# Attention scores, probabilities and AV in plain fp32 with small array tiles, in a transformer block on one core

## The chip, the cores and the metric

The kernel runs on one core of a Trainium2 chip. The metric is the time of one execution on the device in microseconds (us). The profile is one execution as the hardware profiler recorded it.

## The reference

One transformer block on 2,048 tokens of width 448: a layer norm, attention over a sliding window of 256 keys with 16 heads of 28 channels, a residual sum, a second layer norm, and a gated feed-forward layer of width 1,792 with a second residual sum. All inputs and the output are fp32.

```python
def _A_ref(x, wqkv, wo):
    H = 16; Dh = D // H; W = 256
    q, k, v = ...                       # from x @ wqkv
    scores = einsum("bhqd,bhkd->bhqk", q, k) * (Dh ** -0.5)
    mask = (idx[:, None] - idx[None, :] >= 0) & (idx[:, None] - idx[None, :] < W)
    scores = where(mask, scores, -1e9)
    p = softmax(scores, axis=-1)
    o = einsum("bhqk,bhkd->bhqd", p, v)
    return o.transpose(0, 2, 1, 3).reshape(B, S, D) @ wo
x = A_x
h = x + _A_ref(_layernorm(x), A_wqkv, A_wo)
h2 = h + ((gelu(n @ w_gate) * (n @ w_up)) @ w_down)      # n = _layernorm(h)
```

## The kernel before

**Fast fp32 by splitting.** The kernel works in two kinds of matmul. A tile of type F32R is streamed once; to keep fp32 accuracy a value is split into a rounded part ("hi", `to_hi`, on ScalarE) and the rest ("lo", `to_lo`, on VectorE), and a product is the sum of hi x hi, hi x lo and lo x hi. A tile of type F32 is streamed as plain fp32.

**The blocks.** Attention is cut into `NB` = 16 blocks: `B = 4 * c + g`, where c is a chunk of 512 tokens and g one of four groups of four heads. A block has 512 queries and, through the window, up to 768 keys: those of its chunk and the last 256 of the chunk before. The four blocks of the first chunk have no chunk before; they are called first blocks below, the other twelve later blocks.

**What a block does.**

- `project_tile(c, m)` makes q or k of a group for one chunk in 11 split matmuls of 512 columns (L714). Seven tiles m serve four groups, because each tile of 128 columns holds 112 of its own and 16 of the fourth group's k. The result is split by ScalarE and VectorE and written to DRAM by two pairs of DMAs (`put`, L725 and L727).
- `loads(B)` brings q and k back (L747) so that a head has 84 rows: hi and lo parts in three row groups, so that one F32R matmul gives the whole split product. Twelve more rows are zero and eight carry the maxima.
- `scores(B, i, j)` (L765): for query tile i of 128 and head j, one matmul of 84 rows by up to 384 keys; VectorE adds a mask and takes each query's maximum (`most`, L769).
- `maxima(B)` (L796): the maxima are split, transposed by one matmul, and copied by ScalarE into rows 96 to 103 of q, four copies a block (`put`, L424).
- `probs(B, m, o)` (L838): for key tile m the product is computed again, now with keys on the partitions, 104 rows, so that the maximum is subtracted by the matmul; ScalarE takes the exponential into `pp` (L842).
- `select(B, m, o)` (L857): POOL zeroes what the window excludes in the tiles on its edges.
- `attend(B, ms, at)` (L876): AV in plain fp32, 128 rows of keys by 29 columns (28 channels and a column of ones for the sum), four heads side by side in the array at columns 0, 32, 64 and 96, all into one bank.
- `drain(B)` transposes AV on VectorE, divides, transposes back and splits; `output(p, c)` (L936) multiplies two blocks by Wo and adds to `hres`.

`values` (L660) projects v, `layer_norms` prepares the tokens. The feed-forward layer (L1191, L1179, L1386, L1462) follows; its weights are prepared by VectorE, ScalarE, POOL and DMA while attention runs, and its first matmuls (L1191) begin at 265 us.

**The order.** No engine's order is written by hand. Every piece of work is an `op(engine, cost, latency, key, ...)` in a list; `Lists.run` then simulates the engines with these costs, and at each step gives an engine the ready piece with the lowest key (16 keys are one block). It also hands out the eight PSUM banks of 128 x 512: `allowed(kind)` lists the banks that a kind of work may take. Scores use banks 0 and 1, probabilities 2 and 3, AV bank 4, projections and other work 5 to 7. `TURN` is the time that the simulation charges when TensorE changes the tiling of its array. The chip executes the order found; all DMAs go through SP's queue in that order.

Of the kernel before, what the change touches and what calls it, by code (L numbers as in the profile page):

```python
# [16 lines left out]
NT = S // 128  # L17
# [10 lines left out]
PPB = 10  # L28
MERGE = (1, 1, 1, 0, 1, 1, 1, 1, 1, 1, 1, 0)
# [7 lines left out]
LAG_P = 13.5  # L37
LAG_V = 12.0
# [38 lines left out]
PKL = 2  # L77
# [4 lines left out]
PKS = 3  # L82
POOLED = (3,)
PKX = (2, 3)
# [8 lines left out]
TURN = (0.19, 0.09, 0.09)  # L93
# [24 lines left out]
class Lists:  # L118
# [47 lines left out]
    def run(self, allowed, idle):  # L166
# [23 lines left out]
        def start_of(e, o):  # L190
# [6 lines left out]
            for b in o.banks:  # L197
                if b.k is None:
                    ks = [k for k in allowed(b.kind) if bank_free[k] is not None]
# [79 lines left out]
def block_kernel(ctx: ExitStack, tc, x, wqk_in, wv_in, wo_in, gu_in, rest_in, cw_in, down_in, out):  # L279
# [10 lines left out]
    def f(ap):  # L290
# [10 lines left out]
    one_r = pool.tile([128, 128], F32R, name="one")  # L301
# [11 lines left out]
    mx = pool.tile([128, 4, 4], F32, name="mx")  # L313
    mhl = [mhl_m[:, 128 * i:128 * i + 128] for i in range(2)]
    rcp = [pool.tile([128, 16], F32, name=f"rcp{i}") for i in range(2)]

    pool.tile([128, 32], F32, name="pad2")

    qk_d = [[[dram.tile([GF, 3, 512], F32, name=f"{'qk'[i]}{g}_{c}") for i in range(2)] for c in range(CS)]
            for g in range(NG)]  # L320
# [16 lines left out]
    pp_m = lp.tile([128, 4 * PPB * 128], F32, name="pp")  # L337
# [21 lines left out]
    rq = [m.rearrange("p (j t) -> p j t", j=4) for m in rqs]  # L359
    rk = [m.rearrange("p (j t) -> p j t", j=4) for m in rks]  # L360
# [11 lines left out]
    pk = proj_m[:, 3584:5632].rearrange("p (a t) -> p a t", a=4)  # L372
# [3 lines left out]
    wo_raw = raw_m[:, 1024:1472]  # L376

# [7 lines left out]
    def WVRAW(p, b):  # L385
        return span("pp", 7 * p + 1.75 * b, 3.5)
# [3 lines left out]

    def PK(a):
        return span("proj", 3584 + 512 * a, 512)
# [164 lines left out]
    def start():  # L557
# [35 lines left out]
        def const_pick():  # L593
            nc.gpsimd.memset(e8, 0.0)
            for i in range(2):
                nc.gpsimd.affine_select(e8[96:104, 0:4], e8[96:104, 0:4], pattern=[[-1, 4]],
                                        compare_op=OP.not_equal, fill=1.0, base=-4 * i, channel_multiplier=1)

        op("pool", 0.85, 0.9, -100.5, const_pick, (), ["e8"], port=True)
        for i in range(2):  # L600
            op("pool", 0.1, 0.1, -30, lambda i=i: nc.gpsimd.memset(f(mhl[i]), 0.0), (), [("mh", i), ("ml", i)])
        op("act", 0.2, 0.3, -99, lambda: to_hi(one_r, ident), ["ident"], ["one"])

        op("dve", 1.1, 1.15, -99, lambda: nc.vector.memset(f(rqs[0][64:96, 0:1024]), 0.0), (), [("zq", 0, 0)])
        op("act", 1.45, 1.55, -97, lambda: nc.scalar.activation(
            rks[0][64:96, 1536:3072], e8[64:96, 0:1].to_broadcast([32, 1536]), AF.Copy), ["e8"], [("zk", 0, 1)])
# [4 lines left out]
    def constants(after):  # L611
        def const_mask():
            nc.gpsimd.memset(mask, 0.0)
            nc.gpsimd.affine_select(mask[:, 0:128], mask[:, 0:128], pattern=[[1, 128]], compare_op=OP.is_gt,
                                    fill=-BIG, base=0, channel_multiplier=-1)
            nc.gpsimd.affine_select(mask[:, 256:384], mask[:, 256:384], pattern=[[-1, 128]], compare_op=OP.is_ge,
                                    fill=-BIG, base=0, channel_multiplier=1)

        for u, i in ((0, 0), (1, 0), (1, 1)):
            o = 1536 * i  # L620
            op("pool", 1.35, 1.4, (-99, 0)[u], lambda u=u, o=o: nc.gpsimd.memset(f(rks[u][64:96, o:o + 1536]), 0.0), (),
               [("zk", u, i)], after=after)
        for u, i in ((0, 1), (1, 0), (1, 1)):
            o = 1024 * i
            op("pool", 0.95, 1.0, (-98, 0)[u], lambda u=u, o=o: nc.gpsimd.memset(f(rqs[u][64:96, o:o + 1024]), 0.0), (),
               [("zq", u, i)], after=after)
        for u in range(2):
            for j in range(4):
                src = e8[96:104, j:j + 1].to_broadcast([8, 768])
                if j < 2:  # L630
                    op("dve", 0.55, 0.54, (-96, 0)[u] + j, lambda u=u, j=j, src=src: nc.vector.tensor_copy(
                        rk[u][96:104, j], src), ["e8"], [("pick", u, j)], port=True, after=after)
                else:
                    op("act", 0.75, 0.85, (-96, 0)[u] + j, lambda u=u, j=j, src=src: to_hi(rk[u][96:104, j], src),
                       ["e8"], [("pick", u, j)], after=after)
# [43 lines left out]
    pks, ring = [0], [0]  # L679

    def pk_at():
        n = pks[0]
        pks[0] += 1
        if n in PKX:
            m, o, name = pp_m, 1792 + 1024 * PKX.index(n), "pp"
        else:
# [1161 lines left out]
```

## Time and profile before

| | |
|---|---|
| median of 3 runs | 695.22 us (695.12 to 695.36) |
| span of the profiled execution | 693.2 us |
| that execution's own time beside its span | not given; the runs' median stands 2.0 us above the span |
| TensorE busy | 683.7 us |
| VectorE, ScalarE, POOL busy | 540.9, 399.7, 194.2 us |
| matmul records | 5,534 |
| granted TensorE clock | 1.000 |

A row of the profile names a line of the kernel (L765), an engine (PE is TensorE, PEld its weight loads, DVE VectorE, ACT ScalarE, SP the DMA queue), an operation, the tile written and the tiles read, and a shape. `bank<-rk,rq 84*128 84x384 f32 x224 | 72.9, 348` is a group of 224 matmuls with 84 rows and 128 columns of weights and 384 streamed columns, which kept the engine busy for 72.9 us, 348 ns each. A plain fp32 matmul leaves two records for one instruction of the code: AV has 352 matmuls and 704 records. In a timeline a row is a start, a duration and a piece of work; like pieces that follow one another are merged (x8).

### The profile page before, as it was taken

To read this page: it belongs to the slowest core of one execution; us is meant where nothing else is said; L and a number is where in the kernel's file an instruction comes from. 1 tells how busy PE (TensorE), PEld (TensorE's weight loads), DVE (VectorE), ACT (ScalarE), POOL (GpSimd) and SP (SyncE) were. 2 spreads that over 40 slices of the span, in tenths; PEclk is the share of its full clock that TensorE was granted. 3 is DMA by queue.
4 is the path that set the end of the run, shared out by engine and by line. 5 is a ranking of instruction groups with operands and counts; after the bars stand their busy time and mean duration, and the time that the engine had idled before them with its cause. 6 is when DMAs were issued, how large, how long until landed. Compare 5 with 4: busy or idle time off the path is not lost. (4 is left out here: it accounts for less than half of the span.)

```text
span 693.2 us, 15159 instructions
## 1 busy us (share of the span) xinstructions
PE 683.7 (99%) x5534; PEld 581.8 (84%) x5534; DVE 540.9 (78%) x1362; ACT 399.7 (58%) x837; POOL 194.2 (28%) x318
## 2 busy tenths in 40 slices
PE   8999999999999999999999999999999999999997
PEld 7887888887888887878878887888889889999886
DVE  7977678987897798838896899677757888887744
ACT  7747566876677767667554465544524534545430
POOL 5613554644455446441220120010000210120000
PEclk9999999999999999999999999999999999999999
DMA  9997788887789597844754766414103744443102
GB/s 307 286 298 228 240 214 217 191 235 207 192 215 257 130 270 196 213 153 133 192 112 118 213 173 193 129 40 137 60 14 118 226 134 131 133 148 86 43 15 107
DMA packets 104690, 116.24 MB, mean 168 GB/s; under 512 B 44632, under 2 KB 82392, under 8 KB 104040
## 3 DMA queue, kind: packets, MB, share of 16 engines
q1 hardware_dynamic: 104472, 115.17, 59.3%
q8 instruction: 43, 0.70, 0.4%
q14 instruction: 31, 0.25, 0.1%
q10 hardware_dynamic: 144, 0.11, 0.0%
HBM read 84.97 MB, written 44.47 MB: 187 GB/s over the span
## 5 line engine op out<-in xcount | busy, mean ns | idle before, releaser
L769 DVE CUSTOM_DVE_ANT_0 mt<-bank,mt 128x384 bf16<-128x384 f32 (+2 forms) x256 | 126.1, 525 | 23.2 <-PE bank L765 21.0
L1386 PE MATMUL bank<-xT,proj 64*128 64x512 f32 x645 | 121.0, 388 | 0.0
L842 ACT ACTIVATE pp<-bank 128x384 f32<-128x384 f32 (+1 forms) x188 | 90.2, 528 | 17.8 <-PE bank L838 16.7
L1386 PE MATMUL bank<-xo,proj 64*128 64x512 f32 x456 | 98.4, 388 | 0.3 <-DVE e L1302 0.3
L714 PE MATMUL bank<-xT 128*128 128x512 f32 x308 | 95.3, 397 | 0.0
L1386 PEld LDWEIGHTS bank<-xT,proj 64*128 64x128 f32 x645 | 80.9, 184 | 8.9
L838 PE MATMUL bank<-rq,rk 104*128 104x384 f32 (+2 forms) x352 | 80.9, 303 | 0.0
L765 PE MATMUL bank<-rk,rq 84*128 84x384 f32 (+2 forms) x256 | 80.3, 337 | 0.1
L1462 PE MATMUL bank<-proj,gh 64*128 64x448 f32 x624 | 74.9, 362 | 0.0
L857 POOL TENSOR_SCALAR_AFFINE_SELECT pp<-pp 128x512 f32<-128x512 f32 x96 | 60.5, 649 | 44.8 <-ACT pp L842 43.5
L1462 PEld LDWEIGHTS bank<-proj,gh 64*128 64x128 f32 x624 | 62.6, 184 | 6.3 <-DVE e L1302 0.4
L838 PEld LDWEIGHTS bank<-rq,rk 104*128 104x128 f32 x352 | 58.9, 189 | 10.0 <-ACT pp L842 1.7
L1386 PEld LDWEIGHTS bank<-xo,proj 64*128 64x128 f32 x456 | 59.7, 184 | 7.0 <-DVE e L1302 0.7
L714 PEld LDWEIGHTS bank<-xT 128*128 128x128 f32 x308 | 56.2, 189 | 6.8 <-DVE xT L427 0.4
L1386 PE MATMUL bank<-xT,w 64*128 64x512 f32 x276 | 53.8, 389 | 0.3 <-DVE raw L1398 0.3
L424 ACT ACTIVATE rq<-bank 8x512 fp32r<-8x512 f32 x64 | 37.6, 588 | 27.2 <-PE bank L796 26.3
L765 PEld LDWEIGHTS bank<-rk,rq 84*128 84x128 f32 x256 | 46.9, 189 | 6.7 <-DVE mx L769 1.5
L660 PE MATMUL bank<-proj,xT 128*128 128x448 f32 (+1 forms) x220 | 50.6, 334 | 0.3 <-ACT proj L424 0.3
L1386 PE MATMUL bank<-xo,w 64*128 64x512 f32 x240 | 49.7, 391 | 0.7 <-DVE raw L1398 0.6
L1481 DVE TENSOR_TENSOR hres<-bank,hres 128x448 f32<-128x448 f32 (+1 forms) x85 | 47.0, 609 | 1.0 <-PE bank L1462 1.0
L1301 ACT ACTIVATE e<-bank 1x1 f32<-1x1 f32 x75 | 11.8, 158 | 50.0 <-PE bank L1462 34.8
L1386 PEld LDWEIGHTS bank<-xT,w 64*128 64x128 f32 x276 | 35.8, 184 | 4.3 <-DVE raw L1398 0.7
(212 smaller groups left out, 1384.2 us busy)
## 6 DMA issues: line engine op xcount, KB each, us to landing
rk<-k SPq DMA_DIRECT2D x44, 336.0 KB
rq<-q SPq DMA_DIRECT2D x32, 336.0 KB
gu<-in_gu_dram SPq DMA_DIRECT2D x18, 480.0 KB
proj<-gu SPq DMA_DIRECT2D x24, 288.0 KB
q<-proj SPq DMA_DIRECT2D x12, 448.0 KB
proj<-down SPq DMA_DIRECT2D x22, 224.0 KB
proj<-gu SPq DMA_DIRECT2D x24, 192.0 KB
k<-proj SPq DMA_DIRECT2D x9, 448.0 KB
```

Of the source, the lines that this page charges most:

```text
L424: nc.scalar.activation(dst, src, AF.Copy)
L660: op("pe", mm(224 * n), 0.29 if n == 1 else 0.38, key + a / 16, lambda a=a, h=h, wb=wb, xb=xb: nc.tensor.matmul(bank[b.k][:, 0:224 * n], x ...
L714: op("pe", mm(512) + 0.002, 0.403, key, lambda a=a, h=h, wb=wb, xb=xb: nc.tensor.matmul(bank[b.k], wqk[m][:, h, wb, :], xT[:, xb, cc * 128 ...
L765: nc.tensor.matmul(bank[b.k][:, o:384], rq[u][0:3 * DH, j, i * 128:i * 128 + 128], rk[u][0:3 * DH, j, m0 * 128:(i + 3) * 128], start=True, ...
L769: nc.vector.tensor_tensor_reduce(junk[s % 2][:, o:384], bank[b.k][:, o:384], mask[:, o:384], 1.0, -BIG, OP.add, OP.max, mx[:, i, j:j + 1])
L838: nc.tensor.matmul(bank[b.k][:, n * i:n * i + n], rk[u][0:104, j + i, m * 128:m * 128 + 128], rq[u][0:104, j + i, lo * 128:(hi + 1) * 128] ...
L842: nc.scalar.activation(pp_cols(o, n)[:, j:j + G], bank[b.k][:, 0:G * n].rearrange("p (g t) -> p g t", g=G), AF.Exp, scale=SCALE)
L857: nc.gpsimd.affine_select(a, a, pattern=[[0, 4], [-cm, 128]], compare_op=op_, fill=0.0, base=0, channel_multiplier=cm)
L1301: ways = {"act": (0.08, 0.17, lambda: nc.scalar.activation(e8[0:1, 0:1], bank[b.k][0:1, 0:1], AF.Copy), False), "dve": (0.07, 0.17, lambda ...
L1386: nc.tensor.matmul(bank[b.k], w, xarea(u.cp, xl, xs, side)[:, xk], start=p in (1, 2, 5) and not k and not t, stop=t == 2, tile_position=(6 ...
L1462: nc.tensor.matmul(bank[banks[q].k][:, 0:D], h[oh][0]()[HALF[x], q * 128:q * 128 + 128], d[wh][0]()[HALF[x]], start=not ph and not y and n ...
L1481: op("dve", 0.07 + w * 0.463 / D, 0.163 + w * 0.463 / D, key, lambda: nc.vector.tensor_tensor(hres[:, t, c0:c0 + w], bank[b.k][:, c0:c0 + ...
```

## The change

The products of a head stay unsplit. `project_tile` writes q and k straight from the bank into SBUF (`qT[g]`, `kT[g]`, 32 partitions a head: 28 channels and spare rows), by one copy on ScalarE or VectorE, whichever the planner finds free. The trip through DRAM goes; `loads`, `probs`, `slots` and the split of the maxima go with it. The weights are laid out so that each head's 32 columns hold 28 of its own and 4 of the fourth group's k; four DMAs a tile gather those into `kT[3]`, and one fills row 28 of each head with -1.

Scores and probabilities are computed in steps (`scores_and_probs`). A step uses four banks, one a head, of up to 512 columns; a matmul has 32 rows (a head) and 64 columns of weights, at row 32 j and column 64 h, so that eight fit in the array: four heads by two halves of 64 queries or keys. A step holds the scores of one query tile (320 columns in a later block) and the probabilities of an earlier block's group of pieces. VectorE takes maxima and ScalarE exponentials from the same banks. `stage(s)` runs the score steps of block s with probabilities of blocks s - 2 and s - 1, then AV of block s - 2, then `maxima(s)`: VectorE transposes the maxima, four DMAs write them to DRAM and one reads them into q's row 28.

AV is made of matmuls of 64 rows by 29 columns, at row 64 h and column 32 j, with the two halves in two banks; `drain` adds them. `project(B + 2)` is issued two blocks ahead in place of a whole chunk. A step (a "bin" in the code) may take any of the eight banks.

```diff
-    rks = [p.tile([128, 3072], F32R, name=f"rk{u}") for u, p in enumerate((rp, lp))]
-    rqs = [p.tile([128, 2048], F32R, name=f"rq{u}") for u, p in enumerate((rp, lp))]
+    kT = [rp.tile([128, 1024 if g < NG - 1 else S], F32, name=f"k{g}") for g in range(NG)]
+    qT = [lp.tile([128, 512], F32, name=f"q{g}") for g in range(NG)]
...
-TURN = (0.19, 0.09, 0.09)
+TURN = (0.11, 0.11, 0.11, 0.11)
...
     def project_tile(c, m):
...
-        op("act", 0.49, 0.605, key, lambda: to_hi(hl[0], bank[b.k]), (), [tok[0]], b)
-        op("dve", 0.603, 0.698, key, lambda: to_lo(hl[1], bank[b.k], hl[0]), [tok[0]], [tok[1]], b)
...
+        ways = {"act": (0.49, 0.605, lambda: to_hi(dst, bank[b.k]), False),
+                "dve": (0.603, 0.7, lambda: nc.vector.tensor_copy(dst, bank[b.k]), False)}
+        got[B] = op("act", 0.49, 0.605, key, None, (), [main, extra], b, alts=ways)
+        old, new = slice(512 * c, 512 * c + 512), kT[NG - 1]
+        for j in range(4):
+            dma(key + 1, 8, lambda j=j: nc.sync.dma_start(new[32 * j + 4 * m:32 * j + 4 * m + 4, old], dst[32 * j + DH:32 * j + 32]),
+                [extra, "neg"], [("k3", c, m, j)], cost=0.45)
+        if s:
+            dma(key + 2, 8, lambda: nc.sync.dma_start(dst[DH:128:32], new[DH:128:32, old]), ["neg"], [extra], cost=0.45)
...
+    PIECES = {"A": (4, 5, 0, 1, 5), "B": (6, 7, 2, 3, 5), "C": (2, 9, 0, 5, 3), "D": (8, 3, 4, 0, 4), "E": (0, 11, 0, 7, 1),
+              "F": (10, 1, 6, 0, 2), "A1": (4, 5, 0, 1, 3), "B1": (6, 7, 2, 3, 3), "A2": (4, 5, 3, 4, 2), "B2": (6, 7, 5, 6, 2),
+              "d": (8, 9, 4, 4, 4), "f": (10, 11, 6, 6, 2)}
...
+    def scores_and_probs(key, ss, gs):
+        banks = [Bank("bin") for j in range(4)]
...
+        def part(B, h, j, kh, u, n, at, probs):
+            rows = slice(32 * j, 32 * j + DH + probs)
+            dst = HALF[h]
+            if probs:
+                work.append((j, dst, at, n, keys_of(B, kh, 1)[rows], q_of(B)[rows, 64 * u:64 * (u + n)], h))
+                return
+            cuts = [(kh, n)]
+            if block(B)[1] == 2 and B % 4 < NG - 1 and kh < 4 < kh + n:
+                cuts = [(kh, 4 - kh), (4, n - 4 + kh)]
+            for kh, n in cuts:
+                work.append((j, dst, at, n, q_of(B)[rows, 64 * u:64 * u + 64], keys_of(B, kh, n)[rows], h))
+                at += 64 * n
...
+        def go():
+            for j, dst, at, n, w, x, h in work:
+                nc.tensor.matmul(bank[banks[j].k][dst, at:at + 64 * n], w, x, start=True, stop=True,
+                                 tile_position=(32 * j, 64 * h), skip_group_check=True)
+        cost = o * 4 / 2400 + 0.03
+        op("pe", cost, cost + 0.2, key, go, reads, [x for G in gs for x in G.span(0, G.w)], banks, tag="bin", mode=3)
+
+        def most(B, i, o, n, j, hs, b):
+            n, lo = 64 * n, 320 - 64 * n
+            def go():
+                u = B % 2
+                nc.vector.tensor_tensor_reduce(junk[j % 2][hs, lo:320], bank[b.k][hs, o:o + n], mask[hs, lo:320],
+                                               1.0, -BIG, OP.add, OP.max, mx[u][hs, 4 * j + i:4 * j + i + 1])
...
+        def exp(G, o, j, b):
+            op("act", 0.065 + G.w * 0.00088, 0.16 + G.w * 0.00088, key, lambda: nc.scalar.activation(
+                pp[:, j, G.at:G.at + G.w], bank[b.k][:, o:o + G.w], AF.Exp, scale=SCALE), (), [G.span(0, G.w)[j], *ser(b)], b, tag="exp")
...
+    def select(G, key):
...
+        for (ke, ko, ue, uo, n), at in G.pieces:
+            for h, kh, u in ((0, ke, ue), (1, ko, uo)):
+                for v_, cm, op_ in ((kh - 4, -1, OP.is_ge), (kh, 1, OP.is_gt)):
+                    if u <= v_ < u + n:
...
     def maxima(B):
...
+        op("dve", 0.1, 0.2, key, lambda: nc.vector.transpose(mxT[u], mx[u]), al, [("mxT", u)], port=True)
+        for a in range(4):
+            dma(key, 2, lambda a=a: nc.sync.dma_start(mx_d[u][0:16, 32 * a:32 * a + 32], mxT[u][32 * a:32 * a + 16]), [("mxT", u)],
+                [("mxd", u, a)], cost=0.45)
+        dma(key, 8, lambda: nc.sync.dma_start(qT[g][DH:128:32], mx_d[u][0:16].rearrange("(j i) t -> j (i t)", i=4)),
+            [("mxd", u, a) for a in range(4)], [("qx", g)], cost=0.45)
+
+    def stage(s):
+        old = groups[s - 2][-2:] if s > 1 else []
+        new = groups[s - 1] if s else []
...
+        elif s >= 4:
+            part = [G for G in new[:-2] if G.w < 512]
+            todo = [([(s, 0)], old[0:1]), ([(s, 1)], old[1:2]), ([(s, 2)], part[0:1]), ([(s, 3)], part[1:2]),
+                    ([], [G for G in new[:-2] if G.w == 512])]
...
     def attend(B):
...
+            for h, j, kh, lo, hi, o in work:
+                nc.tensor.matmul(bank[banks[h].k][32 * j:32 * j + DH + 1, 64 * lo:64 * hi],
+                                 v[HALF[h], at_v(4 * c - 2 + kh // 2), 4 * g + j, :],
+                                 pp[HALF[h], j, o:o + 64 * (hi - lo)],
+                                 start=(h, j) not in seen_, stop=True, tile_position=(64 * h, 32 * j), skip_group_check=True)
...
     def drain(B):
-        op("dve", 0.63, 0.72, key, lambda: nc.vector.transpose(oblk, bank[b.k]), (), ["oblk"], b)
+        op("act", 0.49, 0.605, key, lambda: to_hi(oblk[:, lo:512], bank[by.k][:, lo:512]), (), ["oblk"], by)
+        op("dve", 0.605, 0.702, key, lambda: nc.vector.tensor_tensor(oT, bank[bx.k], oblk, op=OP.add), ["oblk"], [tok], bx)
+        op("dve", 0.63, 0.72, key, lambda: nc.vector.transpose(oblk, oT), [tok], ["oblk"], port=True)
...
     def allowed(kind):
...
+            return [7, 6, 5, 4] + ([3, 2, 1, 0] if not left["bin"] or kind in ("v", "ln1") and L.fresh("bin") else [])
+        if kind in ("last", "att"):
+            return [5, 4, 3, 2, 1, 0, 6, 7]
+        if kind == "bin":
+            return [0, 1, 2, 3, 4, 5, 6, 7]
```

In `PIECES` an entry names the key units of 64 in the even and the odd half, the first query unit of each, and the number of query units.

More of the change, by code (lines that the diff above doesn't have):

```diff
@@ L198, in start_of @@
                 if b.k is None:
-                    ks = [k for k in allowed(b.kind) if bank_free[k] is not None]
+                    ks = [k for k in allowed(b.kind) if bank_free[k] is not None and k not in [x for _, x in got]]
                     if not ks:
@@ L851, in select @@
[L851 to L862 removed]
+        if kh < 4:
+            c, kh = c - 1, kh + 8
@@ L1679, in free, with project @@
         op("py", 0, 0, 0, lambda: None, (), [name], after=ops)
+    def project(B):
+        c, g = divmod(B, 4)
+        for m in range(2 * g, min(2 * g + 2, WT)):
+            project_tile(c, m)
     ln1(0)
@@ L1742, in block_kernel @@
     down_set(0, 0, DKEY)
-    op("py", 0, 0, 0, open_late, (), ["fp"], after=[o for tag in ("att", "task", "exp", "score", "prob", "most", "tr", "rx") for o in L.all[tag]])
+    op("py", 0, 0, 0, open_late, (), ["fp"], after=[o for tag in ("att", "task", "exp", "bin", "most") for o in L.all[tag]])
     exps.extend(L.all["exp"])
```

453 lines of the change are left out of this document (188 added, 265 removed).

## The prediction

> **What bounds the kernel now.** I read the page from the top: the busy shares, then the slices, then the chain that ended last.
>
> ```profile
> span 693.2 us, 15159 instructions
> ...
> PE 683.7 (99%) x5534; PEld 581.8 (84%) x5534; DVE 540.9 (78%) x1362; ACT 399.7 (58%) x837; POOL 194.2 (28%) x318
> ...
> PE   8999999999999999999999999999999999999997
> ...
> PEclk9999999999999999999999999999999999999999
> DMA  9997788887789597844754766414103744443102
> ```
>
> TensorE is busy from the first slice to the last at full clock, and no other engine comes near. The chain of waits at the end is all feed-forward, which the change leaves alone, so I read attention by stretches instead.
>
> ```profile
> core 0: us, PE busy (x) PEld busy (x) DVE busy (x) ACT busy (x) POOL busy (x), PEclk, DMA share, GB/s
> ...
> 25.00:310.00 285.00, 284.87 (x2022) 234.33 (x2025) 225.59 (x738) 199.11 (x398) 136.01 (x231) 1.00 0.80 220
> ```
>
> A matmul's record holds its latency, so records overlap and "busy" could hide gaps. The timeline of TensorE decides, by start to next start.
>
> ```profile
> 203.72 0.34 PE L838 MATMUL bank<-rq,rk 104*128 104x384 f32 x1
> 203.89 0.84 PE L714 MATMUL bank<-xT 128*128 128x512 f32 x3
> 204.57 0.34 PE L838 MATMUL bank<-rq,rk 104*128 104x384 f32 x1
> 204.75 0.51 PE L765 MATMUL bank<-rk,rq 84*128 84x384 f32 x2
> 205.10 0.34 PE L838 MATMUL bank<-rq,rk 104*128 104x384 f32 x1
> ...
> 205.93 0.40 PE L838 MATMUL bank<-rq,rk 104*128 104x256 f32 x2
> 206.16 0.34 PE L765 MATMUL bank<-rk,rq 84*128 84x384 f32 x1
> ...
> 207.57 0.56 PE L838 MATMUL bank<-rq,rk 104*128 104x128 f32 x4
> 207.97 0.39 PE L765 MATMUL bank<-rk,rq 84*128 84x384 f32 x1
> ```
>
> A score of 384 columns takes 0.175 us (204.75 to 205.10, two of them), a probability matmul of 384, 256 or 128 columns 0.17 (203.72 to 203.89), 0.115 (205.93 to 206.16, two) and 0.10 (207.57 to 207.97, four), a projection of 512 columns 0.23 (203.89 to 204.57, three). 0.17 us for 384 columns and 0.23 for 512 are one pace: the array streams without gaps. So here time is TensorE's work, and the change is worth what it takes from or adds to that work, unless it opens gaps.
>
> **The change, part by part. First what TensorE loses.** The counts are those of the groups with forms kept apart.
>
> ```profile
> L765 PE MATMUL bank<-rk,rq 84*128 84x384 f32 x224 | 72.9, 348 | 0.1
> ...
> L838 PE MATMUL bank<-rq,rk 104*128 104x384 f32 x128 | 43.1, 347 | 0.0
> ...
> L838 PE MATMUL bank<-rq,rk 104*128 104x256 f32 x112 | 22.7, 291 | 0.0
> ...
> L838 PE MATMUL bank<-rq,rk 104*128 104x128 f32 x112 | 16.0, 265 | 0.0
> ...
> L876 PEld LDWEIGHTS bank<-pp,v 128*29 128x29 f32 x512 | 15.5, 108 | 16.5 <-issue 12.9 <-POOL pp L857 0.4 <-POOL bnve L449 0.2
> ```
>
> Scores: 224 x 0.175 = 39.2 us, and 32 shorter ones some 3: 42. Probabilities: 128 x 0.17 + 112 x 0.115 + 112 x 0.10 = 46. The transposed maxima (one matmul a block) 1. AV I take from one block:
>
> ```profile
> 211.19 0.68 PE L714 MATMUL bank<-xT 128*128 128x512 f32 x2
> 211.80 0.42 PE L876 MATMUL bank<-side,v 128*29 128x128 f32 x8
> 212.04 2.34 PE L876 MATMUL bank<-pp,v 128*29 128x256 f32 x32
> 214.19 0.40 PE L876 MATMUL bank<-raw,v 128*29 128x128 f32 x8
> 214.52 0.66 PE L838 MATMUL bank<-rq,rk 104*128 104x128 f32 x4
> ```
>
> The projections end at 211.19 + 2 x 0.23 = 211.65; with the entry 0.15 the block's AV takes 2.87 us to 214.52. Twelve blocks like it and four first ones with nine units of keys instead of twelve: 34.4 + 8.8 = 43. Together TensorE loses 132 us.
>
> **What it gains.** AV is already plain fp32 in four tiles side by side: 32 records over 1,280 columns a head take 212.04 to 214.19, 2.15 us, which is 1.68 ns a column with all four heads at once, four times the 0.45 ns of the split matmuls (0.23 us / 512). The new code does all three products in plain fp32, eight tiles at a time: four heads by two halves. By the code a later block has 20 units of 64 keys by 64 queries in each half, 1,280 columns: scores, probabilities and AV cost 2.15 us each, 6.45 together. A first block has 16 units: 5.16. Sum 12 x 6.45 + 4 x 5.16 = 98 us.
>
> Each change of the tiling leaves the array empty for a moment. On the way in that is the 0.15 us above at most, since one of the two projections may have waited; on the way out eight records of 128 columns take 0.21 (1.68 x 128), to 214.40, and the next starts at 214.52: 0.12. I take 0.12 for each, and 0.03 for eight staggered tiles: a visit costs 0.27. The code has 79 steps of scores and probabilities and 16 AV steps. All apart: 26 us; one visit a stage (17): 5. A step waits for banks that VectorE and ScalarE empty, and projections fit between, so I stay near the upper end: 78 visits, 21 us. TensorE gains 98 + 21 = 119 and loses 132: **13 us less** (8 to 29 by the bounds of the visits).
>
> That eight tiles run side by side no row shows. Nearest rows: four column tiles run fully together (above), and two row tiles in the feed-forward:
>
> ```profile
> 653.24 2.06 PE bank L1386 x18
> 655.30 1.21 PE bank L1462 x12
> ```
>
> 18 half-height matmuls of 512 columns in 2.06 us are 0.114 each, half of 0.23: two row tiles overlap fully. I take full overlap for four by two. The Trainium skill, "TensorE: Matmul & The Clock Gate", section "Measured speedup vs the span model", reports a gain of 10.6 with sixteen 32-row tiles, which speaks for it; no run here shows it.
>
> **The other engines.** VectorE: 224 maxima of 384 keys go to 320 (late blocks 192 of them),
>
> ```profile
> 205.13 0.55 DVE L769 CUSTOM_DVE_ANT_0 mt<-bank,mt 128x384 bf16<-128x384 f32 x1
> ...
> 205.61 0.55 DVE L769 CUSTOM_DVE_ANT_0 mt<-bank,mt 128x384 bf16<-128x384 f32 x1
> ...
> L427 DVE TENSOR_TENSOR proj<-bank,proj 128x512 fp32r<-128x512 f32 x21 | 14.4, 688 | 2.8 <-ACT proj L424 2.7
> ...
> L424 ACT ACTIVATE rq<-bank 8x512 fp32r<-8x512 f32 x64 | 37.6, 588 | 27.2 <-PE bank L796 26.3
> ```
>
> 0.48 us (205.13 to 205.61) by 320/384 is 0.40: 192 x 0.08 = 15 us less, but the first blocks' unequal halves need 96 shorter ones for 64: about 6 back. The 28 low parts (0.69 each, 19 us) go; some 9 projection copies (6 us), 16 adds of the two halves (11 us) and 16 small transposes (2 us) come: about 9 us less of 226, in a stretch some 15 us shorter, 80% busy as before. ScalarE loses the 64 puts (37.6 us) and gains 16 copies (10 us). POOL gets twice as many selects of half the length. None of them sets the end.
>
> Queues: SP loses 112 stores and 76 loads of q and k, and gains four small stores per projection tile (112), 21 fills and 5 transfers a block for the maxima (80): 213 for 188. At 0.45 us each (the four loads in the next fence) that is 11 us more on a queue that is not the bound. But it is served in order: a block's gather waits for four stores to land, and the next blocks' fills, Wo's rows and the feed-forward's weights stand behind it.
>
> The maxima's path is the added wait: before, a matmul and ScalarE's puts; now a transpose, four stores, and a gather. A hop by the nearest row:
>
> ```profile
> 0.79 1.81 SPq L561 DMA_DIRECT2D hres<-in_x_dram  x4
> ...
> 3.33 0.63 DVE L459 BATCH_NORM_STATS2 bnst<-hres 128x6 f32<-128x448 f32 x1 [1.35 <-DMA hres<-in_x_dram]
> ```
>
> 2.5 us from issue to use; two hops and five issues are about 7 us. The probabilities that need them are issued from the third step of the next stage on; a block lasts 285/16 = 17.8 us, of which some half lies between. I cost it at nothing, covered by the next block's projections and first two score steps; without cover it costs up to 7 us a block.
>
> At the start q and k no longer go through DRAM and back, and the DMA engines were at 0.9 or more in the first two slices (the digits above); TensorE's first slice is at 8. A slice is 17 us, so 2 to 3 us are idle there. Gain between 0 and 3 us; I take 2.
>
> **Sum.** 693.2 - 13 - 2 = 678 in the span. The median of the runs, 695.22, stands 2.0 above the span; with it **680 us**.
>
> **The rivals.**
>
> The issue of instructions becomes the bound (slower). Each fp32 matmul gives two load and matmul records; AV now needs 128 pairs in 2.15 us, 17 ns each, and two of five steps 48 pairs in 0.86, 18 ns. The sustained pace shown is 8 records in 0.24 us (211.80 to 212.04), 30 ns, which streaming explains too; for four records there is this:
>
> ```profile
> 162.97 0.13 PEld L876 LDWEIGHTS bank<-pp,v 128*29 128x29 f32 x4 [0.20 <-issue]
> ```
>
> Four loads of 0.108 within 0.13 us start 7 ns apart. If 30 ns is the limit, AV costs 3.84 for 2.15 (+1.7), the two steps 1.44 for 0.86 (+0.6 each), the other three +0.1: 3.2 us a later block, 2.4 a first one, 48 in all: **728**. It decides from about 22 ns on, where AV loses 0.7 and the two steps 0.2 each, 15 us over 16 blocks. The 7 ns speak against it; that no run of more than 8 is shown so close speaks for it. The Trainium skill, "TensorE: Matmul & The Clock Gate", section "Wait — 56ns, not 53.3ns?", states that matmuls start no closer than about 25 ns, however short; by that AV would take 3.2 us and the two steps 1.2, 26 us more, 706. The 7 ns of the trace disagree for different tiles, at least in short bursts.
>
> Waits take the gain: a step needs four banks at once and holds them through four maxima (4 x 0.40) and the exponentials, and the maxima come late by DMA. VectorE's 80% speaks for it. 0.7 us a block is 11: **691**.
>
> The eight tiles run in two turns of four: 98 more, **778**. The two overlaps above speak against it.
>
> More steps joined: with one visit a stage 16 us more go, **664**.
>
> **How the numbers follow.** Forecast (671 to 687) 0.58; waits 0.15; issue 0.15, half of it at 22 to 27 ns a pair (about 695 to 712) and half beyond; two turns 0.03; more joined 0.05; the parts cancel 0.04. 0.2% is 1.4 us, about what a measurement of this kernel tells from no change. Faster: 0.58 + 0.05 + 0.13 of the waits = 0.76; same: 0.04 + 0.01 = 0.05; slower: 0.15 + 0.03 + 0.01 = 0.19. The range runs from 667 to 702: it takes in the waits and the lighter part of the issue rival, and leaves out under 2 in 10.
>
> **What would show it.** Right: TensorE still dense from 25 us on; AV steps near 2.15 us and 512-column steps near 0.86; pauses of 0.10 to 0.12 at each change of tiling; feed-forward's first matmul some 15 us sooner, its own length unchanged. Wrong: AV steps of 3 us or more with all tiles starting late (issue); steps of 1.7 us (two turns); TensorE idle with VectorE's maxima or the gather of q's last row as releaser (waits); feed-forward starting sooner but waiting for its weights' splits.

## The result and the profile after

The changed kernel takes 713.64 us (median of four runs, 712.43 to 716.42) beside 695.17 for the kernel before (694.91 to 695.36) on the same chip: a ratio of 1.0264, with a 95% interval of 1.0237 to 1.0291. The predicted 680.0, and its range up to 702, are missed by 33.6 and 11.6 us. The profiled execution took 712.76 us, its span is 710.9.

The head of the page after, with span, busy time of the engines, and slices:

```profile
span 710.9 us, 22675 instructions
...
PE 692.3 (97%) x9106; PEld 566.4 (80%) x9106; DVE 535.9 (75%) x1409; ACT 361.0 (51%) x864; POOL 205.4 (29%) x430
...
PE   9999999999999989899999999999999999999997
...
PEclk9999999999999999899999999999999999999999
```

TensorE's share has fallen from 99 to 97%, and one digit of the clock is an 8. The same stretch as in the prediction, by engine:

```profile
25.00:310.00 285.00, 275.71 (x5238) 199.81 (x5237) 212.61 (x762) 153.15 (x400) 142.81 (x316) 0.99 0.24 60
```

TensorE was busy for 284.87 of these 285 us before; now it is idle for 9.3, and that is a lower bound, since records overlap. DMA's share fell from 0.80 to 0.24: the trip of q and k through DRAM is gone, and bought nothing at the end.

Where the feed-forward layer's half-row matmuls begin, in the timelines of before and then of after:

```profile
274.18 0.96 PE L1179 MATMUL bank<-xT,proj 64*128 64x512 f32 x6
```

```profile
286.96 0.96 PE L1186 MATMUL bank<-xT,proj 64*128 64x512 f32 x6
```

12.8 us later (its whole-row matmuls, the first of the layer, 10.2 later), where the prediction had some 15 sooner. To see what fills the time I sum, over the whole trace, the time from each matmul's start to the next one's start, by the line of the first:

| TensorE's time, us | before | after |
|---|---|---|
| scores, the maxima's transposes, probabilities, AV of before (L765, L796, L838, L876) | 45.6 + 1.5 + 49.6 + 41.3 = 138.0 | |
| steps of scores and probabilities (L773) | | 101.9 |
| AV (L882) | | 39.6 |
| projections, values, outputs, whole-row feed-forward (L714, L660, L936, L1191; after L659, L626, L944, L1198) | 73.2 + 38.2 + 37.0 + 13.2 = 161.6 | 78.6 + 42.4 + 40.5 + 14.9 = 176.4 |
| the rest of the feed-forward layer | 376.5 | 375.8 |
| start | 10.3 | 11.0 |
| sum of these rows (first to last start 686.2 and 704.4; the rest is rounding) | 686.4 | 704.7 |

138.0 us went, 141.5 came, and 14.8 came on lines that the change does not touch. The rest of the feed-forward layer is as long as before.

One step between projections, in the timeline:

```profile
70.14 1.43 PE L659 MATMUL bank<-xT 128*128 128x512 f32 x5
71.50 0.80 PE L773 MATMUL bank<-k,q 28*64 28x320 f32 x16
72.09 0.53 PE L773 MATMUL bank<-q,k 29*64 29x192 f32 x16
72.55 1.66 PE L659 MATMUL bank<-xT 128*128 128x512 f32 x6
...
239.04 2.56 PE L882 MATMUL bank<-pp,v 64*29 64x192 f32 x128
241.53 0.79 PE L773 MATMUL bank<-k,q 28*64 28x320 f32 x16
```

The step takes 1.05 us (71.50 to 72.55) where 512 columns at 1.68 ns are 0.86; a later block's AV 2.49 (239.04 to 241.53) where 2.15 were expected. Eight tiles do run at once, and 128 AV records in 2.49 us are 19.4 ns each, so an issue rate of 25 or 30 ns a pair is not the bound. The Trainium skill, "TensorE: Matmul & The Clock Gate", section "Wait — 56ns, not 53.3ns?", has matmuls start no closer than about 25 ns; for matmuls in different tiles this row disagrees.

What TensorE's weight loads waited for, largest first (us in total, times, longest; rows by "issue", time with no releaser in the profile, and smaller ones left out):

```profile
PEld bank L773 <- ACT pp L789: 11.4, 33, 0.8
PEld bank L659 <- ACT pp L789: 4.3, 4, 2.3
PEld bank L773 <- DVE mx L783: 2.7, 7, 0.8
PEld bank L882 <- POOL pp L814: 2.3, 5, 0.7
PEld bank L659 <- DVE mx L783: 2.0, 1, 2.0
PEld bank L1198 <- DVE mx L783: 1.9, 1, 1.9
...
PEld bank L773 <- DMA q<-mx: 0.8, 1, 0.8
```

Five of these rows, 22.3 us, are waits for a bank that ScalarE's exponentials (L789) or VectorE's maxima (L783) had not emptied. The trip of the maxima over DMA shows 0.8 us.

### The profile page after: what moved, and what is told of

Its sections match the earlier page's. It is cut to its first block, busy times and chain, and to the rows that moved or that the text cites. A ratio compares the mean times of both kernels' runs of the same rounds, so it can differ in the third digit from the quotient of the medians.

```text
span 710.9 us, 22675 instructions
## 1 busy us (share of the span) xinstructions
PE 692.3 (97%) x9106; PEld 566.4 (80%) x9106; DVE 535.9 (75%) x1409; ACT 361.0 (51%) x864; POOL 205.4 (29%) x430
## 5 line engine op out<-in xcount | busy, mean ns | idle before, releaser
L783 DVE CUSTOM_DVE_ANT_0 mt<-bank,mt 128x320 bf16<-128x320 f32 (+4 forms) x288 | 122.8, 448 | 33.9 <-PE bank L773 18.5
L789 ACT ACTIVATE pp<-bank 128x192 f32<-128x192 f32 (+3 forms) x300 | 99.6, 390 | 75.7 <-PE bank L773 49.3
L814 POOL TENSOR_SCALAR_AFFINE_SELECT pp<-pp 64x256 f32<-64x256 f32 x240 | 96.3, 416 | 60.1 <-ACT pp L789 53.0
L659 PE MATMUL bank<-xT 128*128 128x512 f32 x308 | 83.8, 405 | 5.0 <-ACT pp L789 3.4
L659 PEld LDWEIGHTS bank<-xT 128*128 128x128 f32 x308 | 55.1, 188 | 24.8 <-issue 7.9
L773 PE MATMUL bank<-q,k 29*64 29x128 f32 (+4 forms) x1888 | 61.3, 309 | 1.1 <-DVE mx L783 0.6
L773 PE MATMUL bank<-k,q 28*64 28x320 f32 (+4 forms) x1120 | 57.3, 410 | 0.7 <-ACT pp L789 0.6
L773 PEld LDWEIGHTS bank<-q,k 29*64 29x64 f32 x1888 | 40.6, 131 | 16.3 <-issue 3.2
L626 PE MATMUL bank<-proj,xT 128*128 128x448 f32 (+1 forms) x220 | 46.1, 339 | 0.1
L626 PEld LDWEIGHTS bank<-proj,xT 128*128 128x128 f32 x220 | 35.4, 189 | 7.7 <-issue 3.9
L882 PE MATMUL bank<-pp,v 64*29 64x128 f32 (+4 forms) x1888 | 40.7, 312 | 0.5 <-POOL pp L814 0.3
L882 PEld LDWEIGHTS bank<-pp,v 64*29 64x29 f32 x1888 | 34.2, 106 | 8.5 <-issue 3.7
L773 PEld LDWEIGHTS bank<-k,q 28*64 28x64 f32 x1120 | 23.1, 130 | 21.0 <-ACT pp L789 8.6
```

What stands on the lines that cost most here:

```text
L626: op("pe", mm(224 * n), 0.29 if n == 1 else 0.38, key + a / 16, lambda a=a, h=h, wb=wb, xb=xb: nc.tensor.matmul(bank[b.k][:, 0:224 * n], x ...
L659: op("pe", mm(512) + 0.002, 0.403, key, lambda a=a, h=h, wb=wb, xb=xb: nc.tensor.matmul(bank[b.k], wqk[m][:, h, wb, :], xT[:, xb, cc * 128 ...
L773: nc.tensor.matmul(bank[banks[j].k][dst, at:at + 64 * n], w, x, start=True, stop=True, tile_position=(32 * j, 64 * h), skip_group_check=True)
L783: nc.vector.tensor_tensor_reduce(junk[j % 2][hs, lo:320], bank[b.k][hs, o:o + n], mask[hs, lo:320], 1.0, -BIG, OP.add, OP.max, mx[u][hs, 4 ...
L789: op("act", 0.065 + G.w * 0.00088, 0.16 + G.w * 0.00088, key, lambda: nc.scalar.activation(pp[:, j, G.at:G.at + G.w], bank[b.k][:, o:o + G ...
L814: nc.gpsimd.affine_select(a, a, pattern=[[0, 4], [-cm, 64]], compare_op=op_, fill=0.0, base=0, channel_multiplier=cm)
```

## The experiments

Theory: two costs were sized wrongly, the waits for banks (nothing in the forecast) and the visit to a tiling (0.27 us); the other candidates are the maxima's DMA trip, plain work starved of banks, the order of the work, VectorE and ScalarE taking turns at one bank, and the clock. Where a run's order is "made anew", `Lists.run` found another order from changed costs. Ratios are to the kernel before, measured beside each run, with 95% intervals.

**The visit by itself.** A kernel of TensorE alone, on constant data. `NR` is 12, `plain` a matmul of 128x128 by 512 columns, `sc` one of each of the eight tiles of a step; the functions ending in `_s` do the same in the sorted part. The pattern follows again with AV's eight tiles and with the four tiles of before:

```diff
+    for _ in range(NR):
+        run(3, plain)
+        run(1, sc, 0, 320)
+        run(1, sc, 320, 192)
...
+    run(3 * NR, plain_s)
+    run(NR, sc_s, 0, 320)
+    run(NR, sc_s, 320, 192)
...
```

> Not the computation at all: TensorE alone, on constant data, no eviction; the output is zeros. Twelve turns of three plain 512-column matmuls and one run of tiles stand against the same matmuls sorted (36 plain, then the tiles): the difference by 12 is what one change to a tiling and back costs with no wait in it. Three forms: eight 32x64 tiles of 320 and 192 columns; eight 64x32 tiles, four times 256 columns; four 128x32 tiles, four times 256 columns, as before. If a visit costs what the trace of the changed kernel shows (0.11 in, 0.10 for the first round, 0.09 out, 0.105 for the plain matmul after it), the first two forms give 0.40 us a turn. If it costs the 0.27 us of the prediction and the rest in the trace is waiting, they give 0.27. Issue would show in the sorted part: above 0.86 us for the 32 records of one step and above 2.15 for 128 of AV. At the end TensorE is left idle for one to four pairs of VectorE copies, about 1.2, 2.4, 3.6 and 4.8 us, between stretches of 50 plain matmuls: if an idle stretch near 2 us alone lowers the clock, the first leaves it at 1.00 and the others lower it for some microseconds; if the clock drop in the changed kernel had another cause, it stays at 1.00 after all four.

Its timeline (L54, L65 and L74 are the three tilings in turn with the plain matmuls of L45; L48 plain matmuls sorted; L60, L70, L78 the tilings sorted):

```profile
24.96 1.12 PE L54 MATMUL bank<-k,q 28*64 28x320 f32 x32
26.01 0.96 PE L45 MATMUL bank<-y,w 128*128 128x512 f32 x3
26.90 1.12 PE L54 MATMUL bank<-k,q 28*64 28x320 f32 x32
...
44.27 8.35 PE L48 MATMUL bank<-y,w 128*128 128x512 f32 x36
52.55 10.94 PE L60 MATMUL bank<-k,q 28*64 28x320 f32 x384
63.43 0.97 PE L42 MATMUL bank<-y,w 128*128 128x512 f32 x3
```

A turn takes 1.94 us (24.96 to 26.90). Sorted, three plain matmuls take 8.28 / 12 = 0.69 and a step 10.88 / 12 = 0.907, together 1.597. A visit costs **0.343**: 0.143 within the step (1.05 for 0.907) and 0.20 in the three plain matmuls between (0.89 for 0.69). In the single records the first plain matmul behind the tiles takes 0.335 us to the next start, the second 0.229 and the last, ahead of the tiles, 0.327: so 0.105 of the 0.20 lies behind the tiles and 0.095 ahead of them. The other two tilings:

```profile
89.14 0.96 PE L45 MATMUL bank<-y,w 128*128 128x512 f32 x3
90.03 1.96 PE L65 MATMUL bank<-k,q 64*29 64x256 f32 x64
91.92 0.97 PE L45 MATMUL bank<-y,w 128*128 128x512 f32 x3
...
106.57 20.95 PE L70 MATMUL bank<-k,q 64*29 64x256 f32 x768
127.45 0.96 PE L42 MATMUL bank<-y,w 128*128 128x512 f32 x3
...
130.89 0.96 PE L45 MATMUL bank<-y,w 128*128 128x512 f32 x3
131.78 1.93 PE L74 MATMUL bank<-k,q 128*29 128x256 f32 x32
133.65 0.96 PE L45 MATMUL bank<-y,w 128*128 128x512 f32 x3
...
170.26 20.93 PE L78 MATMUL bank<-k,q 128*29 128x256 f32 x384
191.12 11.63 PE L42 MATMUL bank<-y,w 128*128 128x512 f32 x50
```

AV's: 2.78 a turn less 0.69 and 20.88 / 12 = 1.74: 0.35. The old four tiles: 2.76 less 0.69 and 1.738: 0.33. So a visit has one price for all three, between the two that were expected: 0.345 and not 0.27. The 0.40 that I had read from the changed kernel's trace holds another 0.05, because even sorted a step takes 0.907 and not 0.86.

**Short maxima.**

```diff
-                nc.vector.tensor_tensor_reduce(junk[j % 2][hs, lo:320], bank[b.k][hs, o:o + n], mask[hs, lo:320],
+                nc.vector.tensor_tensor_reduce(junk[j % 2][hs, 256:320], bank[b.k][hs, o + n - 64:o + n], mask[hs, 256:320],
```

> VectorE's maxima read the last 64 columns of each row instead of all 128 to 320, so the maximum over the other keys is left out; nothing else is changed, and every engine's instructions stand in the same order. 288 maxima fall from 0.45 us to about 0.2. If TensorE waits for banks that VectorE and ScalarE empty (some 25 us in the trace), 10 to 25 us go: 689 to 704. If the loss lies in the visits alone, under 2 us go: 711 or more.

702.53 us (701.0 to 703.29), ratio 1.0098 (1.0081 to 1.0115): by the ratios 11.5 us of the 18.4 are gone with less work for VectorE. Who waited for VectorE's maxima (L783) in the changed kernel, and then here:

```profile
  ACT pp L789: 24.2, 48
```

```profile
  ACT pp L789: 5.1, 8
```

The exponentials had waited 48 times for a maximum on the same bank; now 8 times. The five rows of waits above (22.3 us) add up to 15.8 here, 6.5 less: the waits are real. The rest is in part the clock: it is granted at 0.999 to 1.000 in these four runs, and at 0.990 to 0.995 in those of the changed kernel (last section). The run also frees VectorE for its other work (212.6 us busy between 25 and 310 us in the changed kernel, 152.6 here), which it can't tell from the emptying of banks.

**Short maxima and short exponentials.**

```diff
-                pp[:, j, G.at:G.at + G.w], bank[b.k][:, o:o + G.w], AF.Exp, scale=SCALE), ...
+                pp[:, j, G.at:G.at + 64], bank[b.k][:, o:o + 64], AF.Exp, scale=SCALE), ...
```

> As the one with short maxima, and ScalarE's exponentials too take only the first 64 columns of each group (the rest of the probabilities is a constant written once near the start); same order. Banks are emptied in well under half the time. Waits on the emptying: all of the 25 us go, and the drop of the clock that follows one of them: 684 to 692, and what is left above the predicted 680 is visits. Visits alone: 709 or more. Issue of instructions: no change, 712 or more.

700.39 us (699.71 to 702.06), ratio 1.0073 (1.0056 to 1.0091). The groups of the two operations here:

```profile
L783 DVE CUSTOM_DVE_ANT_0 mt<-bank,mt 128x64 bf16<-128x64 f32 (+1 forms) x288 | 57.5, 219 | 56.1 <-PE bank L773 38.8
L789 ACT ACTIVATE pp<-bank 128x64 f32<-128x64 f32 x300 | 51.0, 225 | 93.9 <-PE bank L773 81.7
```

With the work of both about halved (122.8 and 99.6 us in the changed kernel) only 2 us more go by the ratios, whose intervals overlap. Neither theory's number is met: 13 of the 25 have gone, a part of them with the clock (1.000 here), and the kernel is still slower than before. The five rows of waits still add up to 11.0 us. By line of TensorE: steps 91.2, AV 37.9, plain attention lines 174.6.

**Its order made anew** with the costs that the traces show, these short ones included (`TURN` 0.16, steps 0.05 and AV 0.07 longer, select 0.415, maxima 0.22, exponentials 0.225), and any bank for plain work.

> Maxima and exponentials both over 64 columns alone (the rest of both is left out), and the order of the work made anew with the measured costs of everything, these short ones among them. With the old order this computation takes 700 us, about 15 of it still waits. If those 15 stay because the order was made for longer evictions, most of them go: 686 to 693. If they are what is left of each bank's way from TensorE over two engines and back, however it is ordered: 697 to 703.

699.1 us (697.24 to 703.47), ratio 1.0063 (1.0037 to 1.009): the interval overlaps that of the run before it. This second order does not take away what is left.

**Any bank for plain work**, and **the order with measured costs**, both with maxima and exponentials whole:

```diff
-            return [7, 6, 5, 4] + ([3, 2, 1, 0] if not left["bin"] or kind in ("v", "ln1") and L.fresh("bin") else [])
+            return [7, 6, 5, 4, 3, 2, 1, 0]
```

> Projections, values and output products may take any of the eight banks, where the kernel leaves them four while tile steps stand open; the order is worked out anew with that. If the plain matmuls are starved of banks (19 us of idle time ahead of the projections), 4 to 10 us go: 704 to 710. If it is the tile steps that wait, for four banks at once, then plain work in their banks makes it no better: 712 to 718. Visits: no change.

714.7 us (712.24 to 716.07), ratio 1.0264 (1.0241 to 1.0286): nothing gained, so nothing shows that the plain work was starved.

> The same computation; the list that orders the work reckons with the costs that the traces show (a change of tiling 0.16 instead of 0.11 us, a step 0.05 and AV 0.07 us more, a select 0.415), any bank for plain work, and steps 3.0 apart with AV two places and projections some places sooner. If the order was at fault, because it was made with costs too low, a part of the 12 us that the short maxima gave comes back without them: 698 to 706. If the waits lie in VectorE and ScalarE taking turns at each bank, whatever the order: 710 to 716.

715.1 us (714.17 to 718.22), ratio 1.0284 (1.0254 to 1.0314). In this trace the steps take less (97.2 us for 101.9) and the plain attention lines more (181.5 for 176.4): the waits moved.

**Short maxima with the order made anew** for them, any bank for plain work:

> The maxima of the last 64 keys alone, as in the run with short maxima (the maximum over the other keys is left out), and an order worked out anew with the measured costs and with these shorter maxima, any bank for plain work, steps 2.0 apart. Waits: some of the 15 us of waits that stay with short maxima go too, and the drop of the clock does not come back: 690 to 700. Visits alone set the time: no better than 702. With all waits gone the lines of TensorE measured one by one give 138 us removed against 101 at the measured pace, 26 of visits: 684 is the floor.

703.0 us (702.4 to 703.76), ratio 1.0104 (1.0083 to 1.0126): as with short maxima in the old order, and above what the waits theory allowed, where visits alone would leave it. By line, steps and AV take less than in the old order (126.4 us for 133.1), the plain attention lines more (178.8 for 174.9), and the drop of the clock came back: half clock for 3.4 us at 324 us, and a mean of 0.994 to 0.996 in the four runs. It was the version that should have beaten both kernels, and it does not.

**Scores and probabilities in banks of their own.**

```diff
-            scores_and_probs(16 * s + (STEP if len(todo) > 4 else 4) * n, *x)
+            at = 16 * s + (STEP if len(todo) > 4 else 4) * n
+            if x[0]:
+                scores_and_probs(at, x[0], [])
+            if x[1]:
+                scores_and_probs(at + 0.5 * bool(x[0]), [], x[1])
```

> One part of the change undone: scores and probabilities do not share banks, each group of four banks holds only scores (VectorE alone empties them) or only probabilities (ScalarE alone); the order is worked out anew. 38 more runs of tiles, 13 us at 0.345 each. If what costs the 28 us of waits is that VectorE and ScalarE take turns at one bank, most of them go and the sum is 700 to 716. If it is the emptying as such, whoever does it, the waits stay and the visits come on top: 722 to 735.

739.52 us (738.65 to 740.24), ratio 1.0624 (1.0598 to 1.065). What the weight loads waited for:

```profile
PEld bank L773 <- DVE mx L783: 14.9, 41, 1.1
PEld bank L773 <- ACT pp L789: 12.1, 32, 1.4
```

The trace has 108 runs of steps for 70 and 33 more changes from whole matmuls to tiles and back: 38 x 0.143 + 33 x 0.20 = 12 us by the visit's price. 13 more are waits: 27.0 us in these two rows for 14.1. No two engines take turns at a bank any more, and the steps wait longer. So taking turns is not needed for the waits. I put them down to there being more groups of four banks to empty; that is argued, not shown.

**No maximum subtracted.**

```diff
-            rows = slice(32 * j, 32 * j + DH + probs)
+            rows = slice(32 * j, 32 * j + DH)
...
-            reads += [("q", G.B % 4), ("qx", G.B % 4), *k_toks(G.B, True)]
+            reads += [("q", G.B % 4), *k_toks(G.B, False)]
```

> The probabilities are taken without row 28, so no maximum is subtracted; the maxima are still computed, transposed and carried by DMA, but no step waits for them. If the trip of the maxima over two DMAs holds the steps up, 5 to 10 us go (704 to 709). The trace shows 1 us of such waits: by the theory of banks being emptied and of visits no change within 3 us, 711 to 717, from another order of the work.

718.6 us (716.09 to 719.85), ratio 1.032 (1.0286 to 1.0354). The order is another one and 4 us worse, a little over the 3 that I allowed; nothing of the gain that the DMA theory promised. Most of the 4 us is the clock: 0.986 to 0.990 in these runs and 0.990 to 0.995 in the changed kernel's, some 3 us by the means (an estimate: the missing share of the clock times the span). Even with these taken off there is no gain of 5 us, and the trace of the changed kernel showed 0.8 us of such waits: the maxima's trip is covered.

**More visits.** The matmuls of AV's groups with a plain one between them, or the same ones behind:

```diff
+            work.append(None)            # behind each group; the last is dropped
...
+                if x is None:
+                    nc.tensor.matmul(bank[banks[0].k][:, 0:128], wos[0][:, 0, 0, 0:128], wos[0][:, 0, 0, 0:128], start=False, stop=True, skip_group_check=True)
+                    continue
```

> Each AV step is cut into its three to five groups by one plain matmul of 128 columns between groups, added onto the sums: 59 more matmuls, 59 more changes from tiles to whole and back, every other instruction in its order. It is read against the kernel with the same 59 matmuls behind the AV steps. At the visit measured by itself (0.33 to 0.35 us a turn) it is 20 us longer than that one; at the 0.27 us of the prediction 16; if TensorE has idle time in these places that takes the visits in, under 10.

> The same 59 plain matmuls of 128 columns, but all behind the AV step of their block, where plain matmuls follow in most cases: no visit more. 59 times 0.05 (128 columns at the pace of 512 in 0.23) to 0.12 us: 3 to 7 us above the changed kernel, 717 to 721; nothing where TensorE waits for a bank there anyway.

738.65 us (733.8 to 741.22) and 722.55 (720.95 to 723.47), ratios 1.0606 (1.0561 to 1.0652) and 1.0381 (1.0357 to 1.0404): 16.1 us apart. Behind AV the plain matmuls made 8 visits more after all, where a step had followed AV directly (82 stretches of tiles between whole matmuls in place of 74; between, 133), so the 16.1 stand for 51 visits, 0.32 each. The total can't tell this from 0.27: by the intervals the difference is uncertain by some 4 us, and the profiled execution with the matmuls between had half clock for 17.1 us, the other for 10.2, which is worth some 3. Undisturbed blocks are sharper. A block's AV with the matmuls between:

```profile
233.40 0.55 PE L887 MATMUL bank<-pp,v 64*29 64x192 f32 x16
233.88 0.33 PE L884 MATMUL bank<-wos 128*128 128x128 f32 x1
...
237.44 0.79 PE L773 MATMUL bank<-k,q 28*64 28x320 f32 x16
```

4.04 us for 2.49, and the same in ten of the twelve later blocks: 0.39 for each of four insertions, the matmul included. TensorE's idle time takes none of it in. Less the 0.05 to 0.06 of the matmul's own 128 columns (an estimate, at the pace of 512 in 0.23) a visit is some 0.33, near the 0.345 by itself.

## Why the prediction was wrong

**The step that failed** is in the sum: the waits for banks that VectorE's maxima and ScalarE's exponentials empty, which it left at nothing. The runs show some 20 us of them in its place, more than the whole gain of 15 us that it forecast. The prediction had them as a rival, "waits take the gain", at 0.7 us a block (11 us, 691) and a chance of 0.15; the mechanism was the right one, but for the maxima's way over DMA, and its price about half of what came. Against its terms, in TensorE's time by line:

- *Loses 132.* It lost 138.0: 6 us better than forecast. Row counts times durations were close.
- *Gains 98 of streaming.* Confirmed but for 4 us: eight tiles run at 1.77 ns a column in steps (0.907 / 512) and 1.70 in AV (1.74 / 1,024) for 1.68. Two thirds of 98 by 1.77 / 1.68 and one third by 1.70 / 1.68 make 102. That holds for the pieces measured sorted, of 192 to 320 columns; some steps with shorter ones cost more, and what they cost stands in the 28 us below.
- *21 us of visits (78 x 0.27).* The trace has 70 runs of steps and 16 of AV, 12 of them directly behind one another: 86 entries into a tiling, and 74 stretches of tiles between whole matmuls. 86 x 0.143 + 74 x 0.20 = 27. In the kernel before, 12 of the 18 AV runs stood behind a plain line of the table, and their 0.095 each is to be taken off: 26 net, 5 more than forecast. The missing part is the plain matmul behind a visit (0.105): the prediction's way in and way out cover the other two (0.095 and 0.143), but it looked for the price where the next record starts, and not at how much later the one after it starts. Visits explain most of the 14.8 us on lines that the change does not touch: 74 x 0.20 - 12 x 0.095 = 13.7.
- *Waits at nothing.* 141.5 + 14.8 = 156.3 us came; less 102 and 26 there are **28 us** that the prediction did not have. Some 6 of them are the short pieces (below) and 3.4 the slowed clock, so that some 19 are waits; the five rows of weight loads add up to 22.3. With short maxima and short exponentials 14 of the 28 go, and 14 stay (129.1 + 13.0 - 102 - 26); the second order leaves the time about as it was. The prediction named VectorE's 80% as the case for it. That share says little: it is 75% now. What counts, as far as the runs show, is that a step takes four of eight banks and that they must be emptied before a later one can have them.
- *The start, 2 us sooner.* 0.7 us later by the table. Of the terms this is the only one with the wrong sign.

6 better against 4, 5, 28 and 3 worse: 34, the miss of 33.6 within rounding. The 28 are what is left over in this sum, so the sum does not prove them; the rows and the runs above do for the greater part. The rivals of issue and of two turns of four are out by 2.49 us for 128 AV records; the maxima by DMA, half of the waits rival, by the run without the row. "More joined" came true by very little: 74 stretches of tiles for 78 visits, which is worth 1 us.

Even without the 28 us the change would gain little: 102 + 26 against 138 is 10 us, and 4 with the short pieces' some 6. With the price of a visit alone right the forecast would have been about 685 and still on the wrong side.

The last 14 us are not the amount of work on VectorE and ScalarE. The trace explains a part of them. Here is a step of 320 + 128 + 64 columns in the changed kernel:

```profile
233.99 0.79 PE L773 MATMUL bank<-k,q 28*64 28x320 f32 x16
234.58 0.72 PE L773 MATMUL bank<-q,k 29*64 29x64 f32 x32
235.23 1.07 PE L944 MATMUL bank<-wos,ohl 128*128 128x448 f32 x4
```

It takes 1.24 us, in three of the four places where it stands alone, and again with both evictions short; 320 + 192 columns take 1.05. In the same way 128 + 128 + 256 take 1.13, and a later block's AV 2.49 where 1,280 x 1.70 ns + 0.143 are 2.32. These times are the same whatever is emptied, so they are no waits: some 5 us in the later blocks, and some 6 with the first ones (an estimate: the quickest time of each make of step and of AV in the traces, against the sorted pace). The cause of the short pieces' price is open; whether it is their issue no run shows. The other 8 us are still waits: with both evictions short the five rows add up to 11.0. I take these for the fixed part of each bank's way over two engines (219 and 225 ns for 64 columns in the rows above, where 320 and 192 take 0.49 and 0.33), but no run takes that away, and none tries steps of fewer than four banks. The order also differs in all runs where it was made anew, and with it the clock; differences of 4 us between such runs mean nothing.

## What to carry to other kernels

Before trading whole-array matmuls for tiled ones, count the changes of tiling and charge each with what it does to the matmuls ahead of it and behind it as well: here 0.345 us, and with it 26 us of the 36 saved in streaming (138 less 102). When a faster TensorE takes half of the PSUM banks at once, follow one bank from the first matmul to the last reader and ask whether the other half is empty by then; a busy share of 75% on the reading engine says nothing about it. A rival whose mechanism is plain in the code should be priced by such a chain, not by a round number a block.

## What the hardware showed

After some pauses TensorE's granted clock falls to half, and the length of the pause alone does not tell which. In the kernel of visits alone, 50 plain matmuls stand behind idle stretches of 2.43 and 3.62 us:

```profile
218.35 0.50 PE L45 MATMUL bank<-y,w 128*128 128x512 f32 x1 [2.43 <-DVE y L111]
218.69 11.52 PE L42 MATMUL bank<-y,w 128*128 128x512 f32 x50
233.83 0.50 PE L45 MATMUL bank<-y,w 128*128 128x512 f32 x1 [3.62 <-DVE y L111]
234.16 13.15 PE L42 MATMUL bank<-y,w 128*128 128x512 f32 x50
```

They take 11.52 us after the first, at clock 1.00, and 13.15 after the second, where the granted clock is 0.50 from 236 to 238 us. The Trainium skill, "TensorE: Matmul & The Clock Gate", section "What's actually happening", has half clock after an idle window of some 3.4 us; these rows agree. In the changed kernel a pause of 2.09 us left the clock at 1.00, and one of 1.68 us was followed by half clock. Its timeline and its stretches of 2 us (the number ahead of the DMA's is the granted clock):

```profile
254.50 2.11 PE L659 MATMUL bank<-xT 128*128 128x512 f32 x8 [2.09 <-ACT pp L789]
...
292.54 0.96 PE L1198 MATMUL bank<-xT,proj 128*128 128x512 f32 x3 [1.68 <-DVE mx L783]
```

```profile
291.00:293.00 2.00, 0.46 (x2) 0.42 (x3) 1.76 (x8) 1.43 (x8) 1.81 (x3) 1.00 0.57 166
293.00:295.00 2.00, 2.00 (x31) 0.93 (x33) 1.41 (x6) 0.60 (x2) 1.80 (x6) 0.88 0.83 259
295.00:297.00 2.00, 2.00 (x11) 0.83 (x3) 1.71 (x7) 1.21 (x4) 1.60 (x5) 0.50 1.00 288
...
301.00:303.00 2.00, 2.00 (x66) 1.21 (x50) 0.56 (x1) 0.92 (x3) 0.00 (x0) 0.92 0.03 8
```

The half clock begins 2 us after the pause of 1.68 has ended, and lasts 6.8 us; one AV then takes 4.42 us (297.07 to 301.49) in place of 2.49. Ahead of this pause and behind it (from 287.85 and from 293.44 us on) steps come in pieces as their banks come free. What decides between the two pauses no run here isolates. So a wait for a bank can cost more than itself: 6.8 us at half clock are 3.4 us lost (an estimate: TensorE was busy all the while), and of the 9.7 us between the profiled executions of the changed kernel and of the one with short maxima, that had no such drop, these are a third. Over all four runs of each the clock is 0.990 to 0.995 against 0.999 to 1.000, and some 5 of the 11.5 us are this (an estimate: the missing share of the clock times the span).
